# Another order for the items of phase one: pooled attention and a snake MLP on one NeuronCore

## The chip, the cores and the metric

The kernel runs on one core of one Trainium2 chip. The metric is device time in microseconds (us) of one execution. The median of three runs of the kernel before is 902.97 us (902.47, 902.97 and 906.02).

## The reference

Two stages, all in fp32. The first is attention over pooled keys, the second an MLP whose middle function is "snake".

```
k_p, v_p = mean of k, v over 8 neighbouring rows      # 8 x 8 x 576 x 64 -> 8 x 8 x 72 x 64
scores = q @ k_p.T / 8 ; scores -= max(scores)
attn = exp(scores) ; attn /= sum(attn) + 1e-9
x = (attn @ v_p), heads side by side                  # 4608 x 512
h = x @ w_in                                          # 4608 x 2048
g = h + sin(alpha*h)**2 / (alpha + 1e-9)
out = g @ w_out                                       # 4608 x 512
```

## The kernel before

The kernel works in two phases. Phase one computes the attention of the 8 batches and, beside it, h and g; it writes g to a DRAM tensor (`g_bridge`). Phase two reads g back and multiplies it by w_out (L1312). The change touches phase one alone.

Phase one cuts the 4608 tokens into 9 units of 512 and the 2048 columns of w_in into 4 slices per unit, which gives 36 groups, n = 4u + J. A group forms its part of x @ w_in by a Strassen-Winograd scheme of seven products, M1 to M7, each in 4 parts (M1.0 to M1.3; one part is one call of `product`, L993, a 128x256 matmul that the profile shows as two records). Results gather in PSUM banks b1, b6, b5 and b7 of the group: ACT copies b1 to b6 when M1 is in (item c16) and b6 to b7 when M6 is in (c67), and b5 to SBUF (p5). M2 then adds to b1, M3 to b6, M7 and M4 to b7. DVE adds give the quarters of h (a01, a11, and a00 with its sine), ACT forms sines (s00, s01, s10, s11, L1062) and squares (q00, q01, q1, L1069), DVE adds those (a00, f10, f1, L967), and SyncE stores the group (st, L1117). PSUM has few banks, so the next group's products wait for these items: M5 for p5 or a01, M1 for a00 or f10, M6 for c16, M4 for a11.

In units 1 to 6 M1, and for J = 0, 2, 3 also M5, is itself done by a second Strassen level (items i.a, i.b, i.d, i.e1, i.e5 on TensorE, L1084; i.ca, i.cm, i.cb on ACT; i.ad on DVE), except that group 4, the first of unit 1, has none. Its operands are made on POOL (inner_x, w2_1, w2_5, L949). For the first groups POOL also combines slices of w_in (comb1, comb2, comb3a, comb3b, L829).

Unit u also carries the attention of batch b = u + 1, as items that stand among the group items:

- load_k0, load_k1, load_v, load_q on SyncE, and pool_k0, pool_k1, pool_v, pool_vm on POOL (L289, L309);
- scores0 and scores1 on TensorE, each a burst of matmuls (`two_scores`, L462), into banks that shift0 to shift3 (DVE, L482, L483) empty;
- exp0 to exp3 on ACT (L508, a table load ahead of each stretch of them), norm0 to norm3 on DVE (L514, L515) and POOL (L516), turn0 to turn3 on DVE (transposes `tr<-ex`, L648 to L658);
- move: 16 DMAs `ex<-tr` on SyncE (L668); in unit 0 twelve of them on SyncE (move0) and four on ACT's queue (move1, move2);
- values on TensorE (`all_values`, L757 and L770), with one tiny ACT copy (L764) in its middle, then out0 to out4 on ACT (L684), which write x for the next unit;
- for the next batch qa, qb, qc (DVE transposes `tr<-q`, L375, L378, into the tile `tr` that the moves read) and qd, qe (8 DMAs `q<-tr` each on SyncE, L388), which scores0 and scores1 of the next unit read;
- clean and mark, POOL memsets (L524, L527), and sx0 to sx3 (or sn0 to sn3), DVE sums of x (L957);
- in unit 0 also the end of batch 0: nrest, arest and the rest values (vrest, `values_rest`, L740), which write four banks, one of them the bank that f10 of group 2 reads last.

The order is written out by hand. The dictionary ORDER (L42) holds a number for each item: for a group the kind of the group picks the table (`first0` to `first3` for unit 0, `enter` for group 4, `mid0` to `mid3` for units 1 to 6, `exit` for group 27, `end0` to `end3` for units 7 and 8) and an item stands at 7n plus its number; unit items stand at 28u plus their number, from table `U0` or `U`. The agenda is sorted by these places and each engine gets its instructions in that order, under a manual schedule; waits between engines follow from the data. So only the order within one engine matters, not the size of a number.

```
        where = ORDER[self.kind(n)]
        for m, f in acts.items():
            if m in where:
                self.at(7 * n + where[m], f)
...
        self.agenda.sort(key=lambda x: x[:2])
```

Of the kernel before, what the change touches and what calls it, by code (L numbers as in the profile page):

```python
# [47 lines left out]
    "move": 17.27338305, "clean": 19.78664433, "pool_k1": 19.78672339, "pool_v": 24.10050833, "values": 24.10052961, "out4": 24.10337673,  # L48
    "out0": 24.18334766, "qa": 24.22592283, "out2": 24.40118532, "out3": 24.40151322, "qb": 24.4015542, "k_t": 24.40239578, "sx0": 24.40248374,
    "qc": 24.40725766, "inner_x": 24.40727852, "k_c": 24.40730845, "out1": 24.55343636, "qd": 25.48510798, "qe": 25.82098613, "sx2": 27.0834961,  # L50
    "sx1": 27.1501748, "mark": 27.51730649, "sx3": 29.04697296},
# [12 lines left out]
    "vsum": -0.82128805, "qrest": 0.13122707, "ahead": 0.40563602, "vals": 1.96467451, "score4": 1.96940908, "load_v": 2.08618, "win3": 2.42169,  # L64
# [50 lines left out]
"enter": {  # L115
# [1473 lines left out]
```

## Time and profile before

The profiled execution took 903.11 us; its span, which the profile's times count from, is 901.3 us, so 1.81 us lie around it. The granted TensorE clock was 1.000.

| stretch (us from the span's start) | what runs | length | TensorE busy | DVE | ACT | POOL |
|---|---|---|---|---|---|---|
| 0.00 to 21.30 | loads, batch 0 | 21.30 | 18.87 | 15.53 | 11.57 | 9.13 |
| 21.30 to 84.30 | unit 0 | 63.00 | 63.00 | 39.70 | 43.89 | 54.60 |
| 84.30 to 410.27 | units 1 to 6 | 325.97 | 324.46 | 221.82 | 252.83 | 131.07 |
| 410.27 to 512.78 | units 7 and 8 | 102.51 | 102.51 | 63.77 | 76.31 | 0.17 |
| 512.78 to 901.30 | phase two | 388.52 | 384.20 | 330.74 | 70.53 | 1.98 |

The stretches are windows of the trace; each row gives the window's length and how long each engine was busy within it. A line of a timeline reads: start, time, engine, line, operation, out<-in by the program's tiles, shapes, count, and in brackets the idle time before it and what ended it. A line of the chain reads: start, time, engine, tile, line, count; the chain is the sequence of work and waits that ended last. "SPq" is SyncE's DMA queue. TensorE matmuls overlap a little, so the times of neighbouring lines can add up to more than the distance between them.

### The profile page before, as it was taken

The page shows a single profiled execution, that of the slowest core. Times are in us where ns is not written, and L with a number is a line of the kernel's source. Part 1 is how long each engine was busy: PE and PEld are TensorE (multiplying, and loading weights), DVE is VectorE, ACT ScalarE, POOL GpSimd, SP SyncE. Part 2 cuts the span into 40 slices and gives each one's busy share as a digit, 9 for nine tenths or more (in the row PEclk, how much of TensorE's full clock was granted, in tenths as well). Part 3 has the DMA queues.
Part 4 walks back from the last instruction along what each step waited for, and adds up shares of the span by engine and source line. Part 5 has one row for each costly group of instructions (what it writes and reads, how often), then busy time and mean ns, then how long its engine had stood idle before and what let it go on. Part 6 is the DMA issues. An engine that isn't in the chain of part 4 may idle for free.

```text
span 901.3 us, 18365 instructions
## 1 busy us (share of the span) xinstructions
PE 893.0 (99%) x7146; PEld 819.4 (91%) x7146; DVE 671.6 (75%) x1016; ACT 455.1 (50%) x1073; POOL 196.9 (22%) x235
## 2 busy tenths in 40 slices
PE   8999999999999999999999999999999999999998
PEld 5787888988889888898888999999999999999997
DVE  7576856768576685854466999979798888889895
ACT  5786877868777787776976611211111111111111
POOL 4888723634226344130000000000000000000000
PEclk9999999999999999999999999999999999999999
DMA  9975865767667666548136346261618172533401
GB/s 249 243 197 156 241 186 155 212 194 194 195 170 206 186 195 204 151 133 285 75 134 205 100 150 194 66 190 35 224 30 230 32 199 65 172 93 125 139 15 41
DMA packets 128752, 141.18 MB, mean 157 GB/s; under 512 B 46920, under 2 KB 95704, under 8 KB 128664
## 3 DMA queue, kind: packets, MB, share of 16 engines
q1 hardware_dynamic: 125880, 137.88, 53.0%
q10 hardware_dynamic: 2784, 2.11, 0.9%
q8 instruction: 57, 0.93, 0.4%
q14 instruction: 31, 0.25, 0.1%
HBM read 75.37 MB, written 47.19 MB: 136 GB/s over the span
## 4 chain that ended last, share of the span: by engine, by line
PE 97%; SPq 1%; DMA 1%; DVE 0%; ACT 0%; issue 0%; ACTq 0%; DVEq 0%
PE PS L1312 43%; PE PS L993 40%; PE PS L1084 7%; PE PS L462 2%; PE PS L757 2%; SPq L388 1%; PE PS L770 1%; DMA q<-tr 0%; DMA q<-in_q_dram 0%; PE PS L571 0%; PE PS L550 0%; PE PS L1149 0%; PE PS L434 0%; PE PS L715 0%; PE PS L361 0%
## 5 line engine op out<-in xcount | busy, mean ns | idle before, releaser
L993 PE MATMUL PS<-home,a 128*128 128x256 f32 x968 | 249.8, 382 | 0.0
L993 PEld LDWEIGHTS PS<-home,a 128*128 128x128 f32 x968 | 177.8, 190 | 27.5 <-issue 5.5
L993 PE MATMUL PS<-home,as 128*128 128x256 f32 x728 | 193.7, 381 | 0.0
L993 PEld LDWEIGHTS PS<-home,as 128*128 128x128 f32 x728 | 134.4, 190 | 16.8
L1312 PE MATMUL PS<-s,wb 128*128 128x144 f32 x896 | 119.1, 286 | 0.0
L1312 PEld LDWEIGHTS PS<-s,wb 128*128 128x128 f32 x896 | 113.6, 190 | 0.0
L1069 ACT ACTIVATE s<-s,c 128x256 f32<-128x256 f32 (+1 forms) x216 | 113.4, 581 | 0.0
L1362 POOL TENSOR_TENSOR cc<-cc,cb 128x576 f32<-128x576 f32 x1 | 2.0, 1976 | 482.8 <-DVE cb L1267 482.8
L967 DVE TENSOR_TENSOR h<-PS,s 128x512 f32<-128x512 f32 x72 | 48.8, 685 | 69.5 <-ACT s L1069 68.8
L1448 ACT COPY PS<-PS 128x144 f32<-128x144 f32 x56 | 14.7, 263 | 144.1 <-PE PS L1312 141.2
L1312 PE MATMUL PS<-r,wb 128*128 128x144 f32 x512 | 73.2, 286 | 0.0
L1312 PE MATMUL PS<-s,a 128*128 128x144 f32 x512 | 73.2, 286 | 0.0
L1062 ACT ACTIVATE s<-h,al 128x256 f32<-128x256 f32 x144 | 64.1, 500 | 16.6 <-DVE h L967 16.5
L967 DVE TENSOR_TENSOR h<-PS,p 128x512 f32<-128x512 f32 x72 | 48.5, 685 | 26.8 <-PE PS L993 20.9
L1062 ACT ACTIVATE s<-PS,al 128x256 f32<-128x256 f32 x144 | 60.2, 473 | 14.8 <-PE PS L993 14.4
L1312 PEld LDWEIGHTS PS<-r,wb 128*128 128x128 f32 x512 | 67.1, 190 | 0.1
L1312 PEld LDWEIGHTS PS<-s,a 128*128 128x128 f32 x512 | 67.0, 190 | 0.0
L289 POOL TENSOR_TENSOR kvin<-kvin 96x768 f32<-96x768 f32 (+3 forms) x42 | 65.1, 1551 | 4.5 <-DMA kvin<-in_k_dram 2.2
L967 DVE TENSOR_TENSOR h<-h,s 128x1024 f32<-128x1024 f32 x36 | 45.3, 1259 | 27.5 <-ACT s L1069 27.5
L1430 ACT COPY PS<-PS 128x144 f32<-128x144 f32 x56 | 14.7, 263 | 88.6 <-PE PS L1312 88.6
L516 POOL TENSOR_TENSOR ex<-ex,sm 128x576 f32<-128x576 f32 (+1 forms) x28 | 35.2, 1282 | 95.2 <-DVE sm L515 95.0
L1312 PE MATMUL PS<-x,wb 128*128 128x144 f32 x384 | 54.9, 286 | 0.0
(217 smaller groups left out, 1512.2 us busy)
## 6 DMA issues: line engine op xcount, KB each, us to landing
g_bridge<-h SPq DMA_DIRECT2D x72, 512.0 KB
r<-g_bridge SPq DMA_DIRECT2D x31, 1152.0 KB
out_dram<-o SPq DMA_DIRECT2D x122, 72.0 KB
kvin<-in_k_dram SPq DMA_DIRECT2D x14, 576.0 KB
q<-in_q_dram SPq DMA_DIRECT2D x7, 1024.0 KB
kvin<-in_v_dram SPq DMA_DIRECT2D x14, 512.0 KB
ex<-tr SPq DMA_DIRECT2D x54, 92.0 KB
ex<-tr SPq DMA_DIRECT2D x54, 88.0 KB
```

What stands on the lines that cost most here:

```text
L289: self.nc.gpsimd.tensor_tensor(out=t[..., 0:w] if w > D else out, in0=t[..., 0:w], in1=t[..., w:2 * w], op=OP.add)
L462: nc.tensor.matmul(ps[e][r0 + r:r0 + r + q.shape[-1], h, :], q[s], kb[s, hp, :], start=True, stop=True)
L516: nc.gpsimd.tensor_tensor(out=E(i), in0=E(i), in1=sm.unsqueeze(2).to_broadcast([P, n, Sp]), op=OP.mult)
L757: nc.tensor.matmul(o[r:r + 64], w, x, start=start and i < 2, stop=False, skip_group_check=True)
L967: add = lambda o, x, y: nc.vector.tensor_tensor(out=o, in0=x, in1=y, op=OP.add)
L993: nc.tensor.matmul(ps[:, jj, :], self.A[p][:, kk, f * P:(f + 1) * P], x[:, kk, :], start=start and p not in G.begun, stop=(kk == 1), skip_ ...
L1062: self.nc.scalar.activation(out=G.s()[:, i, jj, j, :], in_=src[:, jj], func=AF.Sin, scale=self.al[:, f:f + 1])
L1069: self.nc.scalar.activation(out=x, in_=x, func=AF.Square, scale=self.c[:, f:f + 1])
L1084: nc.tensor.matmul(out, W[m][:, G.J], self.X2[p][m], start=start, stop=True, skip_group_check=True)
L1312: nc.tensor.matmul(out, W[:, J // 2, J % 2, :], A[:, J, :], start=(start and J == 0), stop=(J == self.NJ - 1), skip_group_check=True)
L1430: nc.scalar.copy(out=st["x1"][:, 1, :], in_=st["x1"][:, 0, :])
L1448: nc.scalar.copy(out=x1[:, 0, :], in_=x0[:, 1, :])
```

## The change

Only numbers in ORDER change: in `U`, `U0`, `first0` to `first3`, `enter`, `mid0` to `mid3`, `exit` and `end0` to `end3`. The tables `F` (the start), `U7` and `R` (loads for phase two) stay. No item is added or removed, and none goes to another engine; each engine has as many instructions as before, and ACT loads its tables 19 times in both.

What it makes of the order, by engine, at the places that the prediction speaks of:

| place | engine | before | after |
|---|---|---|---|
| units 1 to 5 | SyncE | store of group J=2, qd, qe | qd, store, qe |
| units 1 to 5 | ACT | p5 (J=3), values' copy, s01 (J=2), c67 (J=3), q01 (J=2), out4 | p5, s01, q01, c67, values' copy, out4 |
| units 1 to 5 | DVE | f10 (J=2), qa, qb, f1 (J=2), sx0, qc | f10, qb, qa, f1, qc, sx0 |
| units 1 to 5 | POOL | pool_vm, clean, pool_k1, pool_v, inner_x, mark | pool_v, pool_k1, clean, pool_vm, mark, inner_x |
| unit 0 | DVE | turn0, turn2, turn3, turn1, f10 (group 1), ..., qc, f10 (group 2), qb, qa | nrest, f10 (group 1), turn0, turn1, turn2, turn3, ..., qc, qa, qb, f10 (group 2) |
| unit 0 | POOL | pool_v, comb2, norm0 to norm3, comb3a, comb3b, w2_1, nrest, ..., inner_x, w2_5 | comb3a, norm0, pool_v, comb2, norm1 to norm3, nrest, w2_1, clean, comb3b, ..., w2_5, inner_x |
| unit 0 | PE | scores1 behind 11 products of group 1; vrest, values | scores1 behind 8 products of group 1; vrest, two products, values |
| unit 1 | DVE | shift1, shift0, shift2, f10 and later f1 (group 3) | shift1, shift0, f1 (group 3), shift2, f10 |
| unit 6 | ACT | p5 (group 27), values' copy, s01, q01 (group 26), c67 | s01, p5, s00 (group 27), q01, values' copy, c67 |

In the other groups parts of the products and ACT's copies, sines and squares trade places with their neighbours. The diff, cut to the tables of the units and some lines of the group tables:

```diff
 "U": {
-    "load_k0": -3.59252, "load_v": -0.96965, "scores0": 2.21711438, "shift1": 8.01878985, "shift0": 8.01879307, "scores1": 8.01896537,
-    "shift2": 8.02007325, "pool_k0": 10.93230799, "shift3": 11.44239931, "exp1": 11.4450007, "exp3": 11.71465795, "exp0": 11.71466216,
-    "exp2": 11.7713791, "norm0": 11.82509327, "norm1": 11.87561963, "norm2": 11.89043148, "norm3": 11.92597283, "turn1": 11.94504945,
-    "turn0": 12.06180375, "turn3": 12.06780465, "load_q": 13.4176, "pool_vm": 13.53121133, "turn2": 13.53822942, "load_k1": 13.54022,
-    "move": 17.27338305, "clean": 19.78664433, "pool_k1": 19.78672339, "pool_v": 24.10050833, "values": 24.10052961, "out4": 24.10337673,
-    "out0": 24.18334766, "qa": 24.22592283, "out2": 24.40118532, "out3": 24.40151322, "qb": 24.4015542, "k_t": 24.40239578, "sx0": 24.40248374,
-    "qc": 24.40725766, "inner_x": 24.40727852, "k_c": 24.40730845, "out1": 24.55343636, "qd": 25.48510798, "qe": 25.82098613, "sx2": 27.0834961,
-    "sx1": 27.1501748, "mark": 27.51730649, "sx3": 29.04697296},
+    "load_k0": -3.59252, "load_v": -0.96965, "scores0": -0.7155662, "shift1": 4.77057214, "shift0": 4.86755319, "scores1": 8.43215141,
+    "pool_k0": 9.71818727, "shift2": 9.92172597, "exp1": 10.32516579, "shift3": 11.45840065, "exp2": 11.4669947, "exp3": 11.80740642,
+    "exp0": 11.82588184, "norm0": 11.87721873, "norm1": 11.87894746, "norm2": 11.88314927, "norm3": 11.88984869, "turn1": 11.8984958,
+    "turn0": 12.6412639, "turn3": 12.64678046, "load_q": 13.4176, "pool_v": 13.50682786, "turn2": 13.52997419, "load_k1": 13.54022,
+    "pool_k1": 17.12173738, "move": 22.37628319, "clean": 22.66396303, "qb": 22.78471276, "qa": 23.50189934, "pool_vm": 23.51338513,
+    "values": 23.55148069, "out4": 24.02383944, "out0": 24.07885458, "qc": 24.10488419, "out2": 24.1483368, "out3": 24.30907334, "sx0": 24.31020081,
+    "mark": 24.353556, "k_t": 24.39010385, "qd": 24.41040623, "inner_x": 24.42561687, "out1": 24.42561879, "k_c": 24.43337005, "qe": 24.43360824,
+    "sx1": 24.45142464, "sx2": 24.49199676, "sx3": 28.03504366},
 "U0": {
-    "vsum": -0.82128805, "qrest": 0.13122707, "ahead": 0.40563602, "vals": 1.96467451, "score4": 1.96940908, "load_v": 2.08618, "win3": 2.42169,
-    "pq0": 2.61176632, "pq3": 2.94120136, "pq1": 2.94591477, "win2": 2.94801, "sx2": 3.49767266, "pq4": 3.69418409, "pq2": 5.85963666,
-    "qt0": 5.86045217, "exp4": 5.86046857, "qt1": 5.8604768, "sx3": 5.86924271, "kt0": 6.20676493, "kc0": 6.30132028, "scores0": 6.90682147,
-    "shift0": 6.91252877, "comb1": 6.9857032, "pool_vm": 6.99552018, "shift1": 7.00074692, "pool_v": 7.02398274, "qt3": 7.40035061, "qt2": 7.41673132,
-    "comb2": 10.91091434, "qt4": 11.3245658, "exp1": 11.74548905, "scores1": 11.95415263, "exp0": 13.19875943, "shift2": 13.24260484,
-    "norm0": 13.24264369, "shift3": 14.76087104, "norm1": 15.70016708, "load_k0": 16.01154, "exp2": 16.32735491, "exp3": 16.43790646,
-    "load_q": 16.43872, "norm2": 16.59866484, "norm3": 16.65682944, "load_k1": 16.66341, "turn0": 17.01506997, "turn2": 17.04830223,
-    "turn3": 17.20982546, "turn1": 17.20982611, "comb3a": 17.50481106, "comb3b": 17.63430935, "w2_1": 17.74803633, "move1": 17.74811255,
-    "move2": 17.80420855, "move0": 23.94130931, "nrest": 24.13067954, "qc": 24.19439752, "pool_k0": 24.30597083, "arest": 24.33359335,
-    "clean": 24.37015018, "qb": 24.40946777, "qa": 24.41474252, "vrest": 24.41521379, "values": 24.41527305, "out0": 24.41565366, "out2": 24.42108396,
-    "sn0": 25.10802076, "out4": 26.14696375, "qd": 26.16971794, "qe": 26.36695784, "pool_k1": 26.45292387, "out3": 26.45363911, "kt1": 26.47337699,
-    "out1": 26.48265382, "sn1": 26.48281628, "mark": 26.65478265, "kc1": 26.70067217, "inner_x": 26.92240747, "sn2": 27.09140652, "w2_5": 36.01864122,
-    "sn3": 39.87575987},
+    "vsum": 0.04685888, "qrest": 1.12609462, "ahead": 1.12621108, "vals": 1.97815979, "score4": 1.98087872, "pq0": 2.00419756, "load_v": 2.08618,
+    "win3": 2.42169, "sx2": 2.42182973, "pq1": 2.4218397, "pq3": 2.42184588, "pq4": 2.83730758, "pq2": 2.86092876, "qt0": 2.93906498,
+    "qt1": 2.94740825, "win2": 2.94801, "comb1": 5.72392355, "pool_vm": 5.72395348, "kt0": 5.72399228, "sx3": 5.72479439, "kc0": 6.21524513,
+    "scores0": 6.59317736, "shift0": 7.14132119, "shift1": 7.16512112, "qt3": 10.42219779, "qt2": 10.42227468, "qt4": 11.04472879,
+    "scores1": 12.20886497, "exp0": 12.23595857, "exp1": 14.92464316, "shift2": 14.9278502, "load_k0": 16.01154, "comb3a": 16.20814587,
+    "norm0": 16.29776801, "pool_v": 16.4221108, "shift3": 16.42214839, "exp2": 16.42215296, "exp4": 16.42215769, "comb2": 16.42215883,
+    "exp3": 16.43105819, "norm1": 16.43167428, "norm2": 16.4386205, "load_q": 16.43872, "norm3": 16.44046597, "nrest": 16.44046722,
+    "w2_1": 16.61364428, "turn0": 16.65937632, "turn1": 16.65967345, "load_k1": 16.66341, "turn2": 16.67489442, "turn3": 16.6813079,
+    "clean": 16.90960681, "move0": 17.46587218, "comb3b": 21.29579239, "move2": 21.30385281, "move1": 21.30620725, "arest": 22.91094756,
+    "qc": 23.11289149, "qa": 23.96501159, "pool_k0": 24.16276033, "qb": 24.3599882, "vrest": 24.40722372, "values": 25.53012284, "out0": 25.53026901,
+    "qd": 25.53459911, "pool_k1": 25.54534932, "mark": 25.69593787, "out2": 25.69675784, "out4": 25.70190844, "qe": 25.72362859, "out1": 26.93478736,
+    "kt1": 26.95040763, "sn0": 26.96227298, "out3": 27.13914838, "sn2": 27.13915109, "kc1": 27.25527689, "w2_5": 27.26652232, "sn1": 28.44198883,
+    "inner_x": 32.84603817, "sn3": 39.88593935},
 "first1": {
...
-    "M4.0": 9.6439487, "s01": 9.65740959, "M4.1": 9.65959006, "s10": 10.20982911, "q1": 10.20988117, "f10": 10.51351842, "q01": 10.76757951,
...
+    "s11": 9.43882656, "M4.1": 9.44046412, "s10": 9.44046688, "q1": 9.53670384, "f10": 9.61110713, "s01": 9.68325803, "q01": 10.84597715,
...
 "first2": {
...
-    "M4.0": 10.0159783, "s11": 10.19131482, "M4.1": 10.22568292, "s10": 10.22660264, "q1": 10.28507387, "q01": 10.30642903, "f10": 10.3446236,
...
+    "M4.3": 9.83058454, "M4.1": 9.96397493, "s01": 9.96515171, "s10": 10.02484838, "q1": 10.21298672, "q01": 10.40614765, "f10": 10.40626298,
...
 "mid2": {
...
-    "q00": -0.44465868, "p5": -0.44334366, "a00": -0.44046992, "M7.0": -0.44018093, "M7.1": -0.43995966, "M7.2": -0.43978457, "M3.2": -0.43954416,
...
-    "M4.1": 5.78673303, "a01": 5.83571973, "M4.3": 6.00232327, "s10": 8.84027852, "q1": 8.85456364, "f10": 10.10048188, "s01": 10.10074389,
-    "q01": 10.10114216, "f1": 10.40238311, "st": 10.81798284},
...
+    "i.e1": -0.7305477, "i.e5": -0.70509466, "c16": -0.56977682, "M6.2": -0.54955232, "p5": -0.54725822, "M6.0": -0.52504911, "M6.1": -0.4701966,
...
+    "a01": 6.94895636, "s11": 7.2613973, "M4.3": 7.31546502, "s10": 7.32244866, "q1": 7.32306914, "s01": 8.50279923, "f10": 8.74402786,
+    "q01": 9.49108473, "f1": 9.51471435, "st": 10.42561803},
 "mid3": {
...
-    "p5": 3.10049025, "M6.2": 3.10049465, "c67": 3.10083618, "M2.2": 3.40158715, "M2.0": 3.40162425, "M2.3": 3.40207601, "s00": 3.40218766,
...
+    "i.e1": 0.19107687, "c16": 0.32017551, "i.e5": 0.32373482, "p5": 1.029466, "M6.2": 1.07581941, "M6.3": 1.196356, "M6.1": 2.01894862,
+    "M6.0": 2.48641416, "M2.1": 2.49191811, "c67": 2.53896932, "M2.3": 2.7601918, "M2.0": 2.96305866, "M2.2": 3.00311553, "s00": 3.31285839,
...
```

More of the change, by code (lines that the diff above doesn't have):

```diff
@@ L83 @@
 "end0": {
[31 rows of a table removed]
-"enter": {
[7 rows of a table removed]
-"exit": {
-    "i.a": -7.54342806, "i.cm": -7.43978181, "i.ca": -7.43965501, "i.b": -4.06805269, "i.cb": -3.78099533, "i.d": -3.00502798, "i.ad": -1.90058645,
[39 rows of a table removed]
-    "i.a": -3.58611387, "i.ca": -3.44584191, "i.b": -3.37068185, "i.cb": -3.0827724, "i.cm": -2.50194449, "i.d": -2.29664793, "i.ad": -1.13367375,
[7 rows of a table removed]
-    "i.a": 3.43753621, "i.ca": 4.45162718, "i.b": 4.45857708, "i.cb": 4.57945816, "i.d": 4.58004332, "i.cm": 4.58063281, "i.ad": 4.714659,
[7 rows of a table removed]
-    "i.a": -2.17490446, "i.cm": -2.12440064, "i.ca": -1.93552153, "i.b": -1.93492047, "i.cb": -1.53788222, "i.d": -1.27393677, "i.ad": -1.19802808,
[7 rows of a table removed]
-    "i.a": -7.54712801, "i.ca": -7.43943167, "i.cm": -6.28968451, "i.b": -4.07067743, "i.cb": -3.87795176, "i.d": -1.82949097, "i.ad": -1.21465702,
[6 rows of a table removed]
[31 rows of a table added]
+"enter": {
[7 rows of a table added]
+"exit": {
+    "i.a": -7.37321365, "i.cm": -7.02132454, "i.ca": -7.02093731, "i.b": -5.99233993, "i.cb": -3.31151209, "i.d": -1.90212034, "i.ad": -0.23282715,
[39 rows of a table added]
+    "i.a": -3.56642288, "i.ca": -3.55808096, "i.b": -3.5580494, "i.cm": -3.50766697, "i.cb": -3.50735679, "i.d": -2.91852143, "i.ad": -2.55581909,
[7 rows of a table added]
+    "i.a": 3.35597368, "i.ca": 3.45987892, "i.cm": 3.48903327, "i.b": 3.60373565, "i.cb": 4.45666273, "i.d": 4.48526604, "i.ad": 4.58585348,
[7 rows of a table added]
+    "i.a": -2.12758907, "i.cm": -2.12688532, "i.ca": -2.06935431, "i.b": -2.04827361, "i.cb": -1.48320566, "i.d": -1.35951347, "i.ad": -1.23762451,
[7 rows of a table added]
+    "i.a": -7.27190921, "i.cm": -7.02422763, "i.ca": -6.68455856, "i.b": -6.26530535, "i.cb": -4.57260556, "i.d": -1.57761861, "i.ad": -0.10929413,
[6 rows of a table added]
 }
```

173 rows, old and new, of the table ORDER are left out of this document.

## The prediction

> **What bounds the kernel now.** I read the page's busy times and its chain first, then the windows of the stages, then the waits and the timelines around each place where TensorE stood still.
>
> ```profile
> PE 893.0 (99%) x7146; PEld 819.4 (91%) x7146; DVE 671.6 (75%) x1016; ACT 455.1 (50%) x1073; POOL 196.9 (22%) x235
> ...
> PE 97%; SPq 1%; DMA 1%; DVE 0%; ACT 0%; issue 0%; ACTq 0%; DVEq 0%
> ```
>
> TensorE is busy 99% of the span and 97% of the chain is its own work. The windows by stage (us, then busy time and count on PE, PEld, DVE, ACT, POOL, granted clock, DMA share, GB/s) say where the rest lies:
>
> ```profile
> 21.30:84.30 63.00, 63.00 (x516) 51.10 (x515) 39.70 (x69) 43.89 (x89) 54.60 (x51) 1.00 0.81 207
> 84.30:410.27 325.97, 324.46 (x2785) 281.60 (x2783) 221.82 (x378) 252.83 (x572) 131.07 (x165) 1.00 0.65 185
> 410.27:512.78 102.51, 102.51 (x477) 90.27 (x477) 63.77 (x94) 76.31 (x170) 0.17 (x1) 1.00 0.47 163
> 512.78:901.30 388.52, 384.20 (x3136) 383.98 (x3135) 330.74 (x437) 70.53 (x222) 1.98 (x1) 1.00 0.41 118
> ```
>
> The reordered stretch runs from 21.30 to 512.78. TensorE lacks nothing there but 325.97 − 324.46 = 1.51 us. Whatever order the same instructions stand in, no more than about that (plus a little time inside bursts that wait) can be won; everything else can only be lost. The lack sits in the second score burst of a unit, which waits for the last q DMAs:
>
> ```profile
> 149.03 0.83 PE L462 MATMUL PS<-kblk,q 64*64 64x72 f32 x34
> 151.02 0.99 PE L462 MATMUL PS<-kblk,q 64*64 64x72 f32 x46 [1.15 <-DMA q<-tr]
> ...
> 94.39 1.46 PE PS L462 x78
> 205.42 1.71 PE PS L462 x78
> 260.28 1.65 PE PS L462 x78
> 315.04 1.46 PE PS L462 x77
> ```
>
> The burst beginning at 149.03 ends near 151.94, 2.9 us, where an undisturbed one takes 1.46 on the chain; so about 1.4 us are lost there, and 0.25 and 0.19 in the two after it. The chain also names the length of a product: L993 takes 102.50 us for 474 records, 0.216 each, two to a product, so one product, called M here, is 0.432 us. By that I count positions.
>
> **The change, part by part.** Instruction counts are the same on every engine, table loads included, and no operation is added or removed. So the cost lies only in who stands behind whom.
>
> *q's way in units 1 to 5 (a gain).* SyncE before: store of the group J=2 at 135.26, then 16 q DMAs that wait for qc (136.54) and run 11.50 us, the last landing 3.40 after its issue.
>
> ```profile
> 135.26 0.87 SPq L1117 DMA_DIRECT2D g_bridge<-h  x2
> 136.57 11.50 SPq L388 DMA_DIRECT2D q<-tr  x16
> ```
>
> Now ACT has q01 of that group before c67, so its f1 on DVE runs at about 132.9 behind qb and qa, and qc follows directly, ending near 134.75. The first eight DMAs start then, 1.8 us earlier, the store (0.87 and two gaps of 0.1) stands between them and the last eight, and the last lands 1.8 − 1.1 = 0.75 earlier. The waits at units 3 and 4 (0.19, 0.12 visible) vanish. Bounds: nothing gained but these two, −0.3, if the store waits longer; −1.7 if all three go. What DMAs stand behind the store is a value load of the next unit, which has 90 us.
>
> *The values burst in units 1 to 5 (a loss).* Its second half of rests (L757, 64x64) must wait until ACT's tiny copy (L764) has read the bank:
>
> ```profile
> 130.44 0.65 PE L757 MATMUL PS<-ex,vm 64*64 64x512 f32 x6
> ...
> 132.41 0.66 PE L757 MATMUL PS<-ex,vm 64*64 64x64 f32 x6
> ```
>
> ```profile
> 129.74 0.59 ACT L968 COPY p<-PS 128x512 f32<-128x512 f32 x1
> 131.69 0.16 ACT L764 COPY order<-PS 128x1 f32<-128x1 f32 x1 [1.36 <-PE PS L757]
> 131.74 0.91 ACT L1062 ACTIVATE s<-h,al 128x256 f32<-128x256 f32 x2
> 132.55 0.59 ACT L968 COPY PS<-PS 128x512 f32<-128x512 f32 x1
> 133.07 0.90 ACT L1069 ACTIVATE s<-s,c 128x256 f32<-128x256 f32 x2
> ```
>
> ACT was idle for 1.36 us there, and the copy was done 0.5 us before it was needed. Now s01, q01 and c67 stand ahead of it: 129.74 + 0.50 (p5) + 0.81 + 0.80 + 0.52 puts the copy at 132.37 and its end at 132.53, against a need at 132.3 to 132.4. With the handing over (0.1) TensorE waits about 0.25, five times: +1.25. Bounds 0 and 2.0 (0.4 each, if ACT is as much later as its own gaps elsewhere). Part of it comes off the q wait behind it: −0.25 in unit 2. In unit 6 (exit) another sine stands there, but the burst itself is a product later; no wait.
>
> *Unit 0 (a loss).* Before, on DVE:
>
> ```profile
> 63.29 0.27 DVE L651 STREAM_TRANSPOSE tr<-ex 128x128 f32<-128x128 f32 x1
> ...
> 76.75 0.69 DVE L967 TENSOR_TENSOR h<-PS,s 128x512 f32<-128x512 f32 x1 [3.87 <-ACT s L1069]
> 77.35 2.36 DVE L375 STREAM_TRANSPOSE tr<-q 128x1024 f32<-128x1024 f32 x2
> ```
>
> The turns ended at 63.55, move0's twelve DMAs ran 63.62 to 71.20, and f10 of group 2 (76.75) came ahead of qb and qa. Now pool_v (3.2) and comb2 (5.1) stand on POOL between norm0 and norm1, so norm3 ends near 62.7 (before 61.26); and f10 of group 1, which waits for its square on ACT until about 61.0, stands ahead of the turns. They end near 65.7, move0 ends at 73.4, and its last two DMAs, issued at 72.2 and 72.8, land by the 3.40 of the q DMA at 75.6 and 76.2; by unit 1, where qa started at 130.50 with the last move DMA issued at about 127.9, in at most 2.6, at 74.8 and 75.4. qa and qb (1.2 each) wait for them and now stand ahead of f10 of group 2, which then ends at 78.7 or 77.9. TensorE reaches the rest values (L740), which write f10's bank, at 79.08 less two products = 78.2. So the wait is 0.5 or none; I take +0.3, bounds 0 and 1.1 (both transposes late by 0.6). Also moved there: f10 of group 2 later delays a00 and a11 of group 3, needed 2 us later.
>
> The Trainium skill, "DMA: Bandwidth & Descriptors", section "Anatomy of one DMA — SWDGE (gpsimd) path", gives a DMA a fixed cost of about 2.0 us, for another path than this one. By it, as an estimate, the moves land at 74.2 and 74.8, f10 waits only for its square, and this term is 0, the sum 0.3 lower; the row of 3.40 speaks against it.
>
> *Small edges.* Where an operand is worked out to come within 0.1 us of its use: scores1 of unit 0 (three products earlier, ACT's copy at 45.6 against 45.5), the inner product of group 5 behind shift2, which f1 of group 3 now delays by 1.2 (97.55 against 97.62), i.b of groups 5, 7, 11, 15, 19, 23 behind ACT's ca. Others have 0.3 to 0.8: c16 of group 2, comb2's second step (56.3 against 57.1, cover 0.8), c16 of group 3, the end groups. Ten edges at 0 to 0.2: +0.5, bounds 0 and 2.0.
>
> *At nothing.* w2_5 ahead of inner_x on POOL makes the latter end near 93.7 instead of 90.09; group 5 wants it at 97.2, a cover of 3.5, beyond which it costs one for one. In the end units ACT has 76.31 of 102.51 us of work, and phase two is untouched: 384 us of matmuls.
>
> Sum: −0.75 − 0.25 − 0.19 − 0.12 + 1.25 + 0.3 + 0.5 = +0.74 on the profiled run of 903.11 (span 901.3 and 1.81 around it) = 903.85; the median of the runs, 902.97, lies 0.14 below it: 903.7.
>
> **Rivals.** *The new waits don't come.* Same gains, no losses: −1.7, 901.3. For it: the margins above are within my error. Against: five values bursts with ACT's copy moved behind three instructions. Faster by over 0.5%, 4.5 us (which is about what a measurement here can tell from none), would need three times the idle time that TensorE has.
>
> *ACT falls behind in every group.* ACT is busy 252.83 of 325.97 us between 84.30 and 410.27, and its copies c16, c67 and ca feed TensorE within the group. If the new order leaves it 0.25 late in each of the 24 groups of units 1 to 6 in place of the ten edges, that is +6.0 in place of 0.5: 909.2. It decides from about 0.2 a group on. Against: the ACT items between c16 and c67 are mostly the same few in another order, and a late copy lets ACT catch up during the next products.
>
> *Unit 0's chain.* Every us by which norm3 or the square of group 1 comes later than worked out delays turns, moves, qa, qb and f10 of group 2; past 0.5 us TensorE pays one for one. 4.5 us would need the turns to end at 70; at 5 us late 908.4. The skill's "TensorE: Matmul & The Clock Gate", section "HAM oscillation — how this bites in real kernels", says that an idle stretch over some 3.4 us halves the clock; that would add to this rival. The trace shows only that the wait of 1.15 left the granted clock at 1.00.
>
> *The order doesn't reach the path:* 903.0, inside the forecast's range.
>
> **How the numbers follow.** Forecast (903.7, own range 902.0 to 905.7) 0.60; no new waits (901.3) 0.18; nothing on the path 0.03; ACT late in every group 0.12; unit 0 long 0.05; something faster that I don't see 0.02. All but the last three lie within 0.5% (898.5 to 907.5). The terms at their good ends give −1.7, at their bad ends −0.3 + 2.0 + 1.1 + 2.0 = +4.8, which would be 907.8; the range 901.3 to 907.0 leaves out the last bit of that and the two slow rivals.
>
> **What would show it.** In the profile after: the burst near 149 to 152 with a wait of some 0.4 in place of 1.15; the values bursts of units 1 to 5 (3.6 us) longer by 0.25, released by ACT's L764; the copy right behind c67; unit 0's move0 beginning near 65.8 and L740 with a wait of 0 to 1; i.b waiting on ACT by tenths. Wrong it would be if window 84.30 to 410.27 shows more than 4 us of TensorE idle, or if a wait over 2 us stands before 90 us.

## The result, and the profile after

The changed kernel takes 907.41 us in the median of 22 runs, the kernel before 903.96 in 22 runs beside it. The ratio is 1.0033, with a 95% interval of 1.0024 to 1.0043: slower by 3.0 us, a third of a per cent, and still "within 0.5%". On the scale of the prediction's 902.97 us that is 906.0, inside its range of 901.3 to 907.0; the 907.41 itself lies above it, but was measured beside a kernel before that took 1 us more than then. The profiled execution took 905.30 us, with a span of 903.5 us against 901.3; it is the third fastest of the 22, 2.1 us below their median. The page of the kernel after, busy times and chain:

```profile
PE 893.7 (99%) x7146; PEld 818.3 (91%) x7146; DVE 682.0 (75%) x1016; ACT 458.1 (51%) x1073; POOL 205.4 (23%) x235
...
PE 91%; DVE 2%; POOL 2%; DMA 2%; ACT 1%; SPq 1%; issue 1%; ACTq 0%; POOLq 0%
```

The instruction counts are as before, but DVE is busy 10.4 us longer (671.6 to 682.0) and POOL 8.5 us (196.9 to 205.4). The same instructions ran longer: that is the first hint. Summed instruction by instruction DVE's work grew by 8.6 us, and two groups account for nearly all of it: the 36 adds f1 (`h<-h,s`, 4.2 us) and the sums of x (L957, 4.1 us), both with two operands in SBUF. DVE's adds with an operand in PSUM did not change (0.685 us mean before, 0.684 and 0.686 after). The chain, which was 97% TensorE, now passes through DVE, POOL and ACT. TensorE's waits after (total, times, longest):

```profile
PE PS L1084 <- ACT PS L1097: 0.9, 3, 0.4
PE PS L1084 <- DVE ex L483: 0.7, 1, 0.7
PE PS L757 <- ACT p L968: 0.3, 1, 0.3
...
PE PS L757 <- DMA ex<-tr: 0.2, 1, 0.2
```

The wait for q DMAs (1.2 before) is gone, and four new kinds stand in its place.

To see where the time went I take the first product of group 0 as zero (it begins at 21.33 before and 21.45 after) and read when the values burst of each unit ends. The number of products and inner products ahead of it is the same in both kernels up to unit 5; the last column is the end of group 35.

| us after the first product | U0 | U1 | U2 | U3 | U4 | U5 | end of phase one |
|---|---|---|---|---|---|---|---|
| before | 62.59 | 112.82 | 168.90 | 224.02 | 278.81 | 333.56 | 491.45 |
| after | 62.17 | 113.47 | 168.21 | 224.12 | 279.75 | 334.96 | 493.00 |
| gained or lost in the stretch | −0.42 | +1.07 | −1.34 | +0.79 | +0.84 | +0.46 | +0.15 |

So phase one is 1.55 us longer: 1.76 won in units 0 and 2, some 3.3 lost in units 1, 3, 4, 5 and the rest. Phase two's matmuls take 384.36 us in each of the twelve traces of this study. What is left of the difference between the two spans lies ahead of the first product (0.12) and behind phase one (0.53), where nothing was reordered. In the twelve traces the first product begins between 21.2 and 23.6 us and phase two with its tail takes 388.5 to 390.6, so single executions can differ by some 4.5 us outside the reordered stretch; therefore I read the experiments by the time inside phase one. Six of the experiments have one execution each, and phase one varies too: by a wait for q DMAs, 0 to 1.4 us, and by tenths in where DVE meets POOL. So the waits and durations at which an edit aims tell more than its total.

*Unit 1.* Timeline of TensorE, then of DVE and POOL, after:

```profile
98.12 0.49 PE L1084 MATMUL PS<-home,a 128*128 128x128 f32 x2 [0.66 <-DVE ex L483]
```

```profile
94.16 2.20 DVE L967 TENSOR_TENSOR h<-h,s 128x1024 f32<-128x1024 f32 x1
```

```profile
93.44 3.77 POOL L289 TENSOR_TENSOR kvin<-kvin 96x768 f32<-96x768 f32 x2
```

f1 of group 3 stands ahead of shift2, as worked out, but takes 2.20 us and not the 1.2 I had put in; pool_k0 runs on POOL when it starts. i.a of group 5 waits 0.66 us for shift2 (L483) behind it.

*Unit 3.* DVE and POOL before, where f1 of group 12 is over (226.81) when pool_k1 starts:

```profile
225.59 1.22 DVE L967 TENSOR_TENSOR h<-h,s 128x1024 f32<-128x1024 f32 x1
```

```profile
228.67 2.89 POOL L289 TENSOR_TENSOR kvin<-kvin 96x768 f32<-96x768 f32 x2
```

DVE, POOL, ACT and TensorE, after:

```profile
224.69 2.49 DVE L967 TENSOR_TENSOR h<-h,s 128x1024 f32<-128x1024 f32 x1
```

```profile
224.29 3.75 POOL L289 TENSOR_TENSOR kvin<-kvin 96x768 f32<-96x768 f32 x2 [3.09 <-DMA kvin<-in_k_dram]
```

```profile
227.21 0.91 ACT L1062 ACTIVATE s<-h,al 128x256 f32<-128x256 f32 x2 [1.00 <-DVE h L967]
...
233.65 0.57 ACT L1097 COPY PS<-PS 128x512 f32<-128x512 f32 x1 [0.50 <-DVE h L967]
```

```profile
234.28 0.49 PE L1084 MATMUL PS<-last,q 128*128 128x128 f32 x2 [0.36 <-ACT PS L1097]
```

The first two lines after overlap: pool_k1, which now stands ahead of clean, runs from 224.29, and f1 of group 12 from 224.69 takes 2.49 us. The sine s11 of group 13 waits for it, the squares follow, a00 of group 14 on DVE, then ca (233.65, released by DVE), and i.b of group 15 waits 0.36 for ca. The same repeats at groups 16 and 20.

*The values bursts.* ACT after, in unit 3: c67 and, behind it, the copy.

```profile
243.07 0.60 ACT L968 COPY PS<-PS 128x512 f32<-128x512 f32 x1
243.59 0.17 ACT L764 COPY order<-PS 128x1 f32<-128x1 f32 x1
```

The copy ends 2.08 us after the burst's begin (241.68), and the burst takes 3.88 us from first to last matmul in units 2, 3 and 4 in place of 3.70. In unit 3 its second half of rests starts at 243.81, 0.05 after the copy's end. In unit 6 the burst takes 3.82 us in place of 3.48; there the second half starts 0.3 us after the copy's end, so the copy is not what held it, and the cause of these 0.34 us stays open.

*The q DMAs.* SyncE and TensorE, after:

```profile
135.15 4.95 SPq L388 DMA_DIRECT2D q<-tr  x8
140.15 1.12 SPq L1117 DMA_DIRECT2D g_bridge<-h  x2
141.31 6.76 SPq L388 DMA_DIRECT2D q<-tr  x8
...
149.75 1.53 PE L462 MATMUL PS<-kblk,q 64*64 64x72 f32 x80
```

The first eight start 1.4 us earlier than before, but the last is issued no earlier (its issue ends at 148.07 in both), and TensorE comes to its burst 0.7 us later. In this trace the burst runs through in 1.53 us (before 2.98).

### The profile page after: what moved, and what is told of

Its sections match the earlier page's. It is cut to its first block, busy times and chain, and to the rows that moved or that the text cites. A ratio compares the mean times of both kernels' runs of the same rounds, so it can differ in the third digit from the quotient of the medians.

```text
span 903.5 us, 18336 instructions
## 1 busy us (share of the span) xinstructions
PE 893.7 (99%) x7146; PEld 818.3 (91%) x7146; DVE 682.0 (75%) x1016; ACT 458.1 (51%) x1073; POOL 205.4 (23%) x235
## 3 DMA queue, kind: packets, MB, share of 16 engines
q10 hardware_dynamic: 2784, 2.11, 0.9%
## 4 chain that ended last, share of the span: by engine, by line
PE 91%; DVE 2%; POOL 2%; DMA 2%; ACT 1%; SPq 1%; issue 1%; ACTq 0%; POOLq 0%
PE PS L1312 42%; PE PS L993 36%; PE PS L1084 6%; PE PS L757 2%; PE PS L462 2%; DVE h L967 1%; SPq L668 1%; PE PS L770 1%; DMA kvin<-in_k_dram 1%; POOL q L949 1%; ACT s L1062 1%; ACT s L1069 0%; POOL kvin L289 0%; DMA q<-in_q_dram 0%; POOL ex L516 0%
## 5 line engine op out<-in xcount | busy, mean ns | idle before, releaser
L289 POOL TENSOR_TENSOR kvin<-kvin 96x768 f32<-96x768 f32 (+3 forms) x42 | 71.1, 1693 | 18.8 <-DMA kvin<-in_k_dram 15.1
L967 DVE TENSOR_TENSOR h<-h,s 128x1024 f32<-128x1024 f32 x36 | 49.6, 1377 | 30.8 <-ACT s L1069 28.7
L968 ACT COPY PS<-PS 128x512 f32<-128x512 f32 x72 | 41.5, 577 | 33.0 <-PE PS L1084 14.0
```

Source lines behind the costliest of these rows:

```text
L289: self.nc.gpsimd.tensor_tensor(out=t[..., 0:w] if w > D else out, in0=t[..., 0:w], in1=t[..., w:2 * w], op=OP.add)
L967: add = lambda o, x, y: nc.vector.tensor_tensor(out=o, in0=x, in1=y, op=OP.add)
L968: copy = lambda o, x: nc.scalar.copy(out=o, in_=x)
```

## The experiments

Two theories stand against each other for the three waits of i.b. The first: a DVE add with both operands in SBUF (f1, `h<-h,s`) is held up while POOL works on SBUF, and the new order puts pool_k1 and w2_5 beside it. The second: the new order on ACT (cm ahead of ca) makes ca late. Every kernel below changes only numbers of ORDER.

**f1 of group 3 behind shift2.**

```diff
 "first3": {
-    ... "f1": 15.49447877,
+    ... "f1": 17.0,
```

> The changed kernel with f1 of group 3 put back behind shift2 on DVE (one number). In the changed kernel g5's i.a waits 0.66 us for shift2, and f1 stands ahead of it with 2.20 us where I had 1.2. Theory: without f1 ahead, shift2 ends 2.2 us earlier, the wait of L1084 for DVE L483 disappears (TensorE 0.8 us earlier at 98), and as all of unit 1's attention then runs earlier, its moves land earlier and the wait of the values burst near 131 (0.31) goes too; span 0.4 to 1.0 shorter, since part of the wait for q DMAs near 150 may come back. Rival: i.a waits for something that only ends with shift2 by chance; then a wait of 0.4 or more stays before i.a under another name, and the span moves by less than 0.3.

The wait of i.a for shift2 is gone. But i.b of group 5 now waits 0.50 for ca, since ca waits for a00 of group 4, which stands behind the moved f1 (still 1.57 us). Unit 1 ends at 113.34 in place of 113.47, phase one at 492.75. The first half of the expectation held, the gain (0.13 in unit 1, 0.25 in phase one) did not reach the 0.4 expected: moving the instruction only moved the wait.

**w2_5 ahead of mark.**

```diff
 "U0": {
-    ... "w2_5": 27.26652232,
+    ... "w2_5": 25.6,
```

> The changed kernel with w2_5 ahead of mark on POOL (one number), so that it runs in POOL's idle time from 80.2 and POOL is through with pool_k0 before 94. DVE's order is untouched. Theory (DVE's add with both operands in SBUF is slow only while POOL works beside it): f1 of group 3 starts near 94.2 and takes 1.2 us in place of 2.20, and i.a waits under 0.15 in place of 0.66. Rival (it is slow there for another reason, such as the DMAs or ACT): f1 still takes about 2.2 and i.a waits 0.6.

With DVE's order untouched f1 of group 3 takes 1.22 us, and the wait before i.a is gone. Unit 1 ends at 112.60, 0.87 earlier. This is the cause of most of unit 1's loss: POOL's work beside f1, not f1's place alone. Phase one as a whole is not shorter (493.25): in this trace f1 of groups 12, 16 and 20 takes 2.50, 2.76 and 2.27 us, and i.b waits 0.35 to 0.36 three groups on, each time.

**clean ahead of pool_k1.**

```diff
 "U": {
-    ... "clean": 22.66396303,
+    ... "clean": 17.1,
```

> The changed kernel with clean put ahead of pool_k1 on POOL again in units 1 to 6 (one number); clean waits for the last turn, so pool_k1 starts about 4 us later. Theory (POOL beside DVE): f1 of groups 12, 16 and 20 takes 1.2 us in place of 2.49, 2.41 and 2.01, the next sine (s11) starts earlier, with it squares, a00 and ca, and the three waits of i.b for ca (0.36, 0.35, 0.21; TensorE loses 0.52, 0.52 and 0.37 there) fall below 0.1; span 1.0 to 1.4 shorter. Rival (ca is late because cm now stands ahead of it on ACT): the three waits stay at 0.2 or more, span within 0.4.

f1 of groups 12, 16 and 20 takes 1.22 us each time, and no wait of L1084 for ca is left. The line of group 12:

```profile
228.50 1.22 DVE L967 TENSOR_TENSOR h<-h,s 128x1024 f32<-128x1024 f32 x1
```

From the end of unit 2's values to the end of phase one it takes 322.47 us, the changed kernel 324.79, before 322.55: the loss of units 3 to 5 is gone. The whole of phase one is only 0.68 shorter (492.32; 1.0 to 1.4 was expected), because in this trace the wait for q DMAs is back, 1.38 us; the SyncE order is that of the changed kernel. The collision has moved and not vanished: f1 of groups 5, 9, 13, 17 and 21 now takes 2.07 or 2.08 us beside other POOL work, but no matmul waits for it there.

**ca ahead of cm.**

```diff
 "mid3": {
-    "i.a": ..., "i.cm": -7.02422763, "i.ca": -6.68455856,
+    "i.a": ..., "i.cm": -6.268, "i.ca": -6.68455856,
```

> The changed kernel with cm behind ca (and behind the place of i.b) in the groups J=3 of units 1 to 5 (one number). Rival theory (cm delays ca): ca starts about 0.3 earlier, the three waits of i.b shrink by 0.3 each, span 0.8 shorter. Theory of POOL beside DVE: ca waits for DVE's a00 of the group before, whatever stands ahead of it on ACT, so it starts at the same time within 0.1 and the waits of 0.36, 0.35 and 0.21 stay within 0.1; span within 0.3.

Waits before i.b of 0.41 and 0.42 stay at groups 19 and 23. At group 15 there is none, and there f1 of group 12 took 1.21 (POOL's pool_k1 began 0.06 us after it), at the other two 2.45 and 2.27. The second theory falls: the wait follows f1, whichever of cm and ca stands first. Phase one takes 494.45, with a q wait of 0.99 and 0.52 at a values burst.

The traces together give the relation. Left of the arrow f1's time, right of it the wait of i.b three groups on:

| trace | groups 12 → 15 | 16 → 19 | 20 → 23 |
|---|---|---|---|
| before | 1.21 → 0 | 1.21 → 0 | 1.21 → 0 |
| after | 2.49 → 0.36 | 2.41 → 0.35 | 2.02 → 0.21 |
| f1 of group 3 behind shift2 | 2.53 → 0.36 | 2.26 → 0.36 | 2.13 → 0.32 |
| w2_5 ahead of mark | 2.50 → 0.35 | 2.76 → 0.36 | 2.27 → 0.36 |
| ca ahead of cm | 1.21 → 0 | 2.45 → 0.41 | 2.27 → 0.42 |
| c67 behind the copy | 2.00 → 0.20 | 1.22 → 0 | 1.99 → 0.18 |
| unit 0 as before | 2.11 → 0.30 | 2.45 → 0.36 | 1.93 → 0.12 |
| clean ahead of pool_k1 | 1.22 → 0 | 1.22 → 0 | 1.22 → 0 |

In the four traces that are left (further down) f1 takes 1.21 or 1.22 us at all three groups, and i.b waits at none. So in 36 cases i.b waits exactly where f1 took 1.9 us or more.

**c67 behind the copy.**

```diff
 "mid3": {
-    ... "c67": 2.53896932,
+    ... "c67": 2.552,
```

> The changed kernel with c67 of the groups J=3 of units 1 to 5 behind the values burst's copy on ACT (one number), s01 and q01 left ahead of it. Theory (the burst's second half waits for that copy): the copy comes 0.52 us earlier, before it is needed, the values bursts of units 2 to 4 take 3.70 again in place of 3.88, and phase one, counted from its first product, is about 0.5 us shorter than the changed kernel's 493.0. Rival (the burst is longer because of its DMAs or bank): still 3.88.

The values bursts of units 3 to 5 take 3.70, as expected for units 3 and 4; unit 2's still takes 3.86, but its second half starts 0.19 us after the copy's end, so something else holds it there. Phase one takes 492.42, 0.58 less than the changed kernel's, with a q wait of 0.75 in it and one of the three i.b waits absent by luck of f1, so this total proves little; the bursts' own times carry it.

**Unit 0 as before.** The tables `U0` and `first0` to `first3` of before in the changed kernel.

```diff
-"U0", "first0", "first1", "first2", "first3": the changed kernel's
+"U0", "first0", "first1", "first2", "first3": those of before
```

> The changed kernel with the tables U0 and first0 to first3 of before, so that only units 1 to 8 are reordered. Theory (unit 0's new order wins 0.4, since two products now stand between vrest and values, and loses 0.8 through f1 of group 3 ahead of shift2): the values burst of unit 0 takes 4.0 again and ends 62.6 after the first product in place of 62.2; no wait of L1084 for DVE L483 near 98; the three waits of i.b for ca (0.2 to 0.4) stay, since they belong to the units' own order. Phase one from its first product 491.9 to 492.9. Rival (unit 0's order is what cost the time): phase one at before's 491.5 or less, and the three waits gone.

Half a miss. The values burst of unit 0 takes 4.06 again and the three waits stay (0.30, 0.36, 0.12), as expected; behind unit 1's values it needs 379.49 us, like the changed kernel (379.53; before 378.63). But phase one takes 495.36: the old unit 0 and the new unit 1 do not fit, and new waits of 0.43 (scores0 for kblk), 0.67 (i.b of group 5) and 0.73 (unit 1's values) stand up to 134 us. Tables tuned together can't be priced one by one by exchanging them.

**Three numbers mended.** w2_5, clean and c67 as above, all in one.

> The changed kernel with three numbers mended: w2_5 ahead of mark, clean ahead of pool_k1, c67 behind the copy. If the three causes are the whole loss, phase one from its first product takes 493.0 - 0.9 - 1.4 - 0.5 = 490.2 (before 491.45), up to 491.6 if the wait for q DMAs near 150 comes back as it did with clean alone; against before 0.9985 to 1.0005. If something else in the new order costs as much, it stays above 492 and the ratio above 1.001.

No wait of L1084 is left, the values bursts take 3.70 to 3.73. Phase one takes 491.07, under before's 491.45 although q waits of 1.42 and 0.26 are in it. Ratio to before 0.9990 (0.9979 to 1.0002). Mending these three places is enough to take the loss away; against before that is no measurable gain, and how the loss divides among the three can't be read from one trace each.

**Two things of the change alone, in the kernel before.**

```diff
 "U0": {
-    ... "vrest": 24.41521379,
+    ... "vrest": 24.41477,
 "mid2": {
-    ... "s01": 10.10074389, "q01": 10.10114216,
+    ... "s01": 10.100500, "q01": 10.100510,
```

> The kernel before with two things of the change alone: s01 and q01 of the groups J=2 ahead of the values copy (c67 stays behind it), so that f1 and qc on DVE and the q DMAs come some 1.5 us earlier in units 1 to 5, and one product between vrest and values in unit 0. Theory (the second score burst waits for DMAs that start too late): the q wait of 1.15 near 150 falls below 0.3, the values burst of unit 0 takes about 3.6 in place of 4.0, the other bursts stay; phase one from its first product 489.5 to 490.2 in place of 491.45; ratio about 0.998. Rival (the q wait is the DMAs' own, it comes and goes whatever the start): a wait near 150 of 0.9 or more stays, phase one 491.0.

The values burst of unit 0 takes 3.48 in place of 4.07: one product between vrest and values is enough, which fits with ACT's copies of vrest (before, 79.94 to 80.51, while the burst begins at 79.86) as what held it. The q DMAs' last issue comes 1.3 us earlier (125.48 after the first product, before 126.74), yet a wait of 0.97 stays. Phase one 490.77; ratio 0.9993 (0.9981 to 1.0005). On q the rival is right, or half of it: an earlier start alone does not take the wait away.

**Four numbers mended.** As three, and the store behind qe.

```diff
 "mid2": {
-    ... "st": 10.42561803},
+    ... "st": 10.434},
```

> The changed kernel with the three numbers mended and, fourth, the store of the groups J=2 behind qe on SyncE in units 1 to 5 (where the change has qd, store, qe). In the looks so far the wait for q DMAs near 150 came and went (0 to 1.4 us) with the store between. Theory (the store's 1 MB, 3 us of all DMA engines at 370 GB/s, lies in front of qe's eight DMAs): qe is issued about 3 us earlier, the wait of L462 for q DMAs falls below 0.3, nothing else changes; phase one from its first product 489.4 to 490.0 in place of 491.07, ratio to before about 0.998. Rival (qe's landing does not depend on the store): a wait of 0.7 or more stays. Or the store's h buffer is freed too late, and DVE's a00 or a01 of group J=0 waits for it.

The q wait is gone in all units (bursts of 1.53), qe ends 123.63 after the first product (with the store between 126.03, so 2.4 us earlier where 3 were expected), phase one takes 489.39. Ratio to before 0.9981, interval 0.9972 to 0.9990: this version is 0.2% faster than before, and so faster than the changed kernel too. TensorE's only wait behind 21 us is one of 0.41 in unit 5's values burst.

**The same in the kernel before.** The two edits above and the store behind qe.

```diff
 "mid2": {
-    ... "st": 10.81798284},
+    ... "st": 11.83},
```

> The kernel before with s01 and q01 ahead of the values copy, one product between vrest and values in unit 0, and third the store of the groups J=2 behind qe. There the store was ahead of qd, and qd waited for qc, which stands behind sx0 on DVE, so the store cost SyncE nothing and its data was through before qe's. Theory of the store's data: the wait of 0.97 near 150 stays within 0.3 of that, phase one 490.5 to 491.0. If the wait vanishes (phase one below 489.9), the store delays q even from in front.

The q wait vanishes here too, though qe is issued to its end no earlier (125.73 after the first product) than with the store in front (125.48, wait 0.97), so there too the store's data had delayed q, as far as one trace of each tells. But the kernel is slower than before, 1.0023 (1.0011 to 1.0035): the store now comes too late, at 149 us, and the next group that uses the same h buffer waits for it. DVE's line in unit 2:

```profile
155.05 0.69 DVE L967 TENSOR_TENSOR h<-PS,s 128x512 f32<-128x512 f32 x1 [1.79 <-DMA g_bridge<-h]
```

TensorE waits 1.24, 0.87 and 0.57 for ca behind the same add in units 2, 3 and 6 (in unit 3 the store lands at 210.77, and an ACT exp that the add waits for too ends at 210.80); phase one takes 493.44. In the four-number version the same store is issued 2.1 us earlier and nobody waits.

## Why the prediction was right, and where it was not

The ratio lies in the range and within 0.5%, and the argument for that held: TensorE had only 1.5 us of idle time in the reordered stretch, so little could be won, and the change moved waits about. TensorE's idle time from 84.30 to 410.27 is 2.3 us after, under the 4 us named as a sign of being wrong. The size was forecast too small: +0.74 us against 3.0, which lies above the forecast's own 902.0 to 905.7. That the total came no further off is partly luck, since the errors of the terms have both signs. From the starts of TensorE's matmuls, stretch by stretch, in the two profiled executions (the measured terms add up to +1.6, phase one to +1.55):

| term | forecast | measured in phase one |
|---|---|---|
| waits of the score bursts for q | −1.31 | −1.96 |
| values bursts | +1.25 | +0.94 |
| unit 0 | +0.3 | −0.42 |
| small edges | +0.5 | +3.06 |

*The values bursts:* mechanism right, a little smaller: 0.18 in units 2 to 4 in place of 0.25 (the copy ended 2.08 us into the burst, 2.09 as worked out, but is needed a little later than I read off); in unit 1 the burst began late itself, in unit 5 it waited for its moves. Some +0.6 in units 1 to 5 in place of +1.25, and +0.34 in unit 6, where I had expected nothing.

*The q DMAs:* right in sign in this trace and larger than forecast (second bursts of units 2 to 4: −1.45, −0.16, −0.19; −1.31 in all was forecast, with 0.19 and 0.12 for units 3 and 4 where the bursts shown were 0.25 and 0.19 too long), wrong in mechanism. The last q DMA was issued no earlier, for the store's 1 MB between qd and qe slowed qe's issues (6.76 us for eight, before 5.03). With the same order the wait came back, at 0.75 to 1.42 us, in four of the eight traces that have it. So the gain in this trace was luck.

*Unit 0:* the layout by hand held to tenths: move0 at 65.36 (forecast 65.8), f10 of group 2 done at 77.77 (77.9 to 78.7), vrest at 78.30 (78.2) with no wait. f10 waited only for its square (0.39 us): qa began at 74.32 and qb right behind it, so the last moves landed before the 75.6 and 76.2 that I took from the row of 3.40. What I did not see was a gain: before, the values burst took 4.07 us, and with two products between it and vrest it takes 3.48. −0.42 in place of +0.3.

*The small edges* are the step that failed. I gave them +0.5 for margins of 0 to 0.2. They cost 1.06 in unit 1 (0.66 of it before i.a of group 5, 0.31 before unit 1's values) and 0.77, 0.85 and 0.38 in units 3, 4 and 5, around the waits of i.b of groups 15, 19 and 23, where some products ahead of the wait stretch too (0.16 of unit 5's is the wait for its moves). The error has one root: I priced f1 at 1.2 us everywhere, though the timeline of before had a line of the same shape beside POOL's work,

```profile
68.84 1.27 POOL L949 TENSOR_TENSOR aM<-a 128x512 f32<-128x512 f32 x1
...
69.03 2.17 DVE L967 TENSOR_TENSOR h<-h,s 128x1024 f32<-128x1024 f32 x1
```

and I put POOL's reordering (clean, pool_k1, w2_5) down "at nothing", asking only when POOL's results are needed and not what they run beside. The Trainium skill, "SBUF — State Buffer", sections "SBUF: two separate sides" and "Who interferes with whom", says that VectorE and GpSimd share a pair of SBUF ports as an exclusive lock, and that a VectorE operation with two SBUF inputs and a GpSimd operation that reads SBUF hold each other up whole, whichever starts second. The traces agree to a tenth: f1 takes 1.22 us alone, and about 1.08 us more than the rest of POOL's running instruction where it meets one (rest 0.41: 1.50; 0.92: 2.00; 1.41: 2.49; 1.68: 2.76). That rule spoke against this change, and I had not asked it.

Of the rivals, "ACT falls behind in every group" had the right wait (i.b for ca) in the wrong number, three groups and not 24, and not through ACT's order.

What stays open: the two profiled executions lie 2.2 us apart, of which phase one explains 1.55; the other 0.65 lie at the start and in the tail, whose instructions stand in the same order, and are within what those stretches vary by. The medians differ by more than the profiled executions, because the one of the changed kernel is among its fastest. What the typical execution has besides was not traced; a q wait, which four of eight traces with this SyncE order show, would be a candidate. Also open is why one and the same SyncE order shows a q wait of 1.4 in one trace and none in another.

## What to carry to other kernels

When a change moves work on an engine that looks idle, ask what it now runs beside, not only who waits for its result: POOL's place cost more here (some 3 us) than the later copy on ACT (0.6). Where an instruction appears with two durations in one profile, find out what decides between them before pricing it. A store can be moved behind small transfers that something waits for, but for free only as long as its buffer isn't wanted back.

## What the runs showed of the hardware

- A DVE add of two SBUF operands (f1, 128x1024, fp32) takes 1.22 us alone. Beside a POOL tensor operation that was running when it started it takes the rest of that operation plus 1.08 us, up to 2.76 in these traces, while POOL's operation keeps its time (the first of pool_k1's two, 1.81). Where POOL's operation starts after f1, f1 keeps 1.2 and POOL's takes longer (2.83 in place of 1.81 where it began 0.06 us after f1). Adds with one operand in PSUM (128x512) don't change beside POOL: 0.684 us mean of 60 beside it, 0.686 of 84 without, after.
- A store of two DMAs with 1 MB in all fills the 16 DMA engines for 2 to 3 us (142 to 144 us after: share 1.02 and 1.05, 375 and 371 GB/s), and eight small SBUF-to-SBUF DMAs behind it on the same queue took 6.76 us to issue in place of 5.03. Its own landing was 5.42 us after its issue where it held up an add.
